# Two transposes of a round side by side, and weight sums in place, in a fused layer on one core

## The chip, the cores and the metric

The kernel runs on one core of a Trainium2 chip, in one launch. The metric is device time in microseconds (us), the median of three runs. TensorE multiplies matrices, ScalarE and VectorE work elementwise and read its results in PSUM, GpSimd works elementwise on SBUF alone, and SyncE issues most DMAs.

## The reference

The input x has 2048 tokens of 512 features. All matrices are float32.

```python
xn = _layernorm(x, axis=-1)
s = _A_ref(xn, A_wqkv, A_w_phi, A_wo)
g = _silu(_B_ref(xn, B_W_gate, B_W_up, B_W_down))
return x + s * g
...
# _A_ref: linear attention, 32 heads of 16; per head a 16x16 matrix w_phi
pq = jnp.einsum("bhsd,hdf->bhsf", q, w_phi)
pk = jnp.einsum("bhsd,hdf->bhsf", k, w_phi)
phi_q = jnp.concatenate([_softmax(pq, axis=-1), _softmax(-pq, axis=-1)], axis=-1)
phi_k = jnp.concatenate([_softmax(pk, axis=-1), _softmax(-pk, axis=-1)], axis=-1)
kv = jnp.einsum("bhsf,bhsd->bhfd", phi_k, v)
z  = jnp.einsum("bhsf->bhf", phi_k)
num = jnp.einsum("bhqf,bhfd->bhqd", phi_q, kv)
den = jnp.einsum("bhqf,bhf->bhq", phi_q, z)[..., None] + 1e-6
...
# _B_ref: (relu(xn @ W_gate) * (xn @ W_up)) @ W_down, 1376 hidden features
```

## The kernel before

**Numbers.** A float32 factor is split into a high part (fp32r, by a ScalarE copy) and a low part (the rest, by a subtraction on VectorE or GpSimd). `mm3` multiplies with three matmuls for each 128 rows: low by high, high by low, high by high. `fold` multiplies the key weights by the block-diagonal `w_phi`, so that one projection gives `pk`.

**Token tiles and rounds.** The 16 tiles of 128 tokens are taken in the order `order`; `pair(m)` is round m, m = 1 to 7, for the tiles n = 2m and n + 1. Around it stand a lead-in (weights, tiles 0 and 1) and the second part of the kernel (gate, up, down, queries, output), which begins at about 142 us and which the diff does not touch. In a round a later tile is normalized (`norm_stats`, `norm_scale`: VectorE and a power on GpSimd; `norm_apply`: a short VectorE operation and a ScalarE pass `xt`), transposed (`turn`: four TensorE transposes into `pxT`, a ScalarE copy of the high part and for an even tile one of the whole, `xf`) and completed (`turned`: VectorE subtracts the low part, and for an odd tile makes two sums `sb`). `sums_more`, `sums_hi` and `sums_lo` make from these the token sums S1 and S3 in `XT`.

**Seven products for eight.** From round 3 on (`FIRST`), the key and value projections of a pair of tiles are computed together as seven block products with sums of tokens and sums of weights (A11, S1, S2, A12, S3, A22, S4, in this order on TensorE). ScalarE copies `pk` to `px`, and TensorE goes on accumulating in `px`. The four weight sums T[0] to T[3] are made in `t_prep` in rounds 1 to 3: `PLAN` says at which place of which round each step runs. In "gc51" the letters are engine (g: GpSimd) and operation (c: combine, h: high part, l: low part), the digits which sum or combination and which half k. T[3] is the tile `th`.

**Order.** Every engine runs its instructions in the order of the program. Generators in `Clock` let out the other work (`q_sums` for the query weights `tq`, the preparations for the second part) when its own estimate of the engines' queues is short; `Q_AT` is the half round in which `q_sums` may begin. Buffers come from pools: `u8` has 2, `u4` 10, `u2` 40 (`t3`, `t4`, `vb`, `xt`, `xf`, `sb` and others), PSUM 8.

Of the kernel before, what the change touches and what calls it, by code (L numbers as in the profile page):

```python
# [19 lines left out]
KD = D // P  # L20
# [14 lines left out]
         *(((q, j), (q + 1, j)) for q in (6, 4) for j in range(2)), ((3, 0), (3, 1))]  # L35
LAST = [2 * q + j for q in QUERIES[1] for j in range(2)][-3:]
AHEAD, AT = (), ()
Q_TILES, Q_AT = ((), (1,)), 7
FIRST, SWAP = 3, 3
PLAN = {(0, "turned"): "gc51", (1, "split b"): "gc50", (1, "sums"): "gc01", (1, "scaled"): "gc11", (1, "mid"): "gc21", (1, "split a"): "gc00 sh01 gl01", (1, "turned"): "gc10", (2, "split b"): "sh20 sh11", (2, "sums"): "sh00 gc20", (2, "scaled"): "sh21 gl00", (2, "split a"): "gl20", (2, "turned"): "sh10 gc30 gl11", (2, "end"): "gl21 gl10", (3, "start"): "gc31 gc40 gc41", (3, "split b"): "sh30", (3, "sums"): "sh31 gl30 gl31"}  # L40

START = (14, 15)
TURN = 9
KV_AT = (2,4,6)
SUMS = 5
WO_WITH = (4, 5, 6, 7)
# [131 lines left out]
def layer_kernel(ctx: ExitStack, tc: tile.TileContext, x, wkT, wqT, wv, wo, wf, cst, out):  # L178
# [31 lines left out]
    def f32(t):  # L210
        return t.bitcast(F32)

    def add(engine, o, a, b, op=ALU.add):
        engine.tensor_tensor(o, a, b, op=op)
# [4 lines left out]
    def split(hi, lo, src, lo_engine=None):  # L219

        nc.scalar.activation(hi, src, AF.Copy)
        add(lo_engine or nc.vector, lo, src, f32(hi), ALU.subtract)
# [36 lines left out]
    def even_first(t):  # L259

        return t.rearrange("p (m a f) -> p a m f", a=2, f=DH)

    def by_parity(t):
        return t.rearrange("p (a m f) -> p a m f", a=2, f=DH)
# [19 lines left out]
    def fold(w, raw, k):  # L284

        p = ps(name="pfold")
        for j in range(KD):
            mm(p[:, j * P:(j + 1) * P], raw[:, j * P:(j + 1) * P], bd_sb[:, j, :], j == 0, True)
        return lambda: split(*map(by_parity, w[k]), even_first(p))


    mhalf = sb.tile([P, 96], F32, name="mhalf")[:, 0:2]
# [91 lines left out]
    def turned(n, p):  # L384
        lo_xt(n, p)
        if n % 2:
            sums_x(n, p)
# [1076 lines left out]
    def wv_lo(k):  # L1464
        add(nc.gpsimd, by_parity(WV[k][1]), even_first(wv_raw[:, k, :]), f32(by_parity(WV[k][0])), ALU.subtract)
# [22 lines left out]
    norm_vector_apply(1)  # L1488
    pk = project(0, WK, "pk")
    folds = fold_queries(0, 1)  # L1490
    for k in range(2):
        wv_hi(k)
        wv_lo(k)
    early = exponents(pk)
    folds[0]()
    folds[1]()
# [23 lines left out]
    def t_prep():  # L1520

        def four(name, whole, dt=F32R):
            if whole:
                t = u4((P, 2, D), name, dt)
                return [t[:, k] for k in range(2)]
            return [u2((P, D), name, dt) for k in range(2)]
        raw = [even_first(wv_raw[:, k, :]) for k in range(KD)]
        t3, t4, pairs = four("t3", False, F32), [], {}

        def source(i, k):  # L1530
            return raw[k + 2 * i] if i < 2 else by_parity((t3, t4)[i - 2][k])

        def combine(engine, k, i):
            if i == 5:
                add(engine, by_parity(t3[k]), raw[k + 2], raw[k], ALU.subtract)
            elif i < 2:
                add(engine, raw[k], raw[k], by_parity(f32(WK[k][i])), ALU.subtract)
            elif i == 2:
                add(engine, raw[k + 2], raw[k + 2], raw[k], ALU.subtract)
            else:  # L1540
                if not t4:
                    t4.extend(four("t4", False, F32))
                o, (wh, wl) = t4[k], WK[k + 2]
                if i == 3:
                    add(engine, by_parity(o), by_parity(f32(wh)), raw[k + 2], ALU.subtract)
                else:
                    add(engine, o, o, f32(wl))

        def hi(i, k):
            if i not in pairs:  # L1550
                if i < 3:
                    pairs[i] = list(zip(four(f"h{i}", not i), four(f"l{i}", not i)))
                else:
                    h = u8((P, 2, 2, D), "th", F32R)
                    pairs[i] = [(h[:, 0, j], h[:, 1, j]) for j in range(2)]
                T[i] = pairs[i]
            nc.scalar.activation(by_parity(T[i][k][0]), source(i, k), AF.Copy)

        def lo(engine, i, k):
            add(engine, by_parity(T[i][k][1]), source(i, k), by_parity(f32(T[i][k][0])), ALU.subtract)  # L1560
        def step(what):
            e, op, i, k = what
            engine, i, k = {"v": nc.vector, "g": nc.gpsimd, "s": None}[e], int(i), int(k)
            if op == "h":
                hi(i, k)
            elif op == "l":
                lo(engine, i, k)
            else:
                combine(engine, k, i)
        STEPS.append(step)  # L1570
# [74 lines left out]
    def pair(m):  # L1645

        n, c = 2 * m, cols(2 * m)
        at[0] = n

        def block(p, s, w, first):  # L1650
            mm3(p, lambda k: (XT[:, s, 0, k, c], XT[:, s, 1, k, c]), rows(w), range(2), first)
            pace.pump()
        if m <= NP // 2:
            pace.later(4, lambda: spill_x(n - 1))
        seven = m >= FIRST
        py = ps(name="pk")
        if seven:
            block(py, A11, WK[:2], True)
            px = ps(name="pk")
            nc.scalar.activation(px, py, AF.Copy)  # L1660
        else:
            mm3(py, xt_cols(n), rows(WK), range(KD))
        if m > 1:
            features_k(n - 1, *EB.pop(), engine=MULT[m > SWAP][1])
        t_steps(m, "start")
        pz = ps(name="pv")
        if seven:
            block(pz, S1, T[0], True)
            block(px, S2, T[1], False)
            va = u2((P, D), "va")  # L1670
            nc.scalar.activation(va, px, AF.Copy)
        else:
            mm3(pz, xt_cols(n + 1), rows(WV), range(KD))
        if m == 1:
            norm_apply(n + 4)
        else:
            features_split(n - 1)
        t_steps(m, "split b")
        news = [k for k in (n + 5, n + 6) if k < N]
        if news:  # L1680
            norm_stats(*news, bn=m > 2)
        if seven:
            block(py, A12, WK[2:], False)
        ea = exponents(py)
        if m > TURN and n + 3 < N:
            t = turn(n + 3)
        if seven:
            block(px, S3, T[2], False)
            vb = u2((P, D), "vb")
            nc.scalar.activation(vb, px, AF.Copy)  # L1690
            VH[n + 1] = u2((P, D), "v")
            add(nc.vector, by_head(VH[n + 1], True), by_head(pz), by_head(vb))
        else:
            vb = pz
        t_steps(m, "sums")
        if news:
            norm_scale(*news)
        t_steps(m, "scaled")
        pace.pump()
        at[0] = n + 1  # L1700
        if m <= TURN and n + 3 < N:
            t = turn(n + 3)
        exp_all(ea)
        if not seven:
            features_v(n + 1, vb)
        if n + 3 < N:
            turned(*t)
            sums_more(n + 3)
            sums_hi(n + 3, 0)
            if n + 7 < N:  # L1710
                load_x(n + 7)
        t_steps(m, "mid")
        query(n - 1)
        if m < SUMS:
            features_k(n, ea, py, engine=MULT[m > SWAP][0])
        if n + 3 < N:
            sums_hi(n + 3, 1)
            sums_lo(n + 3)
        if m >= SUMS:
            features_k(n, ea, py, engine=MULT[m > SWAP][0])  # L1720
        for k in news:
            norm_apply(k)
        pace.pump()
        features_split(n)
        t_steps(m, "split a")
        if m in KV_AT:
            kv_products(*range(KV_FROM.pop(), n))
            KV_FROM.append(n)
        pace.pump()
        if seven:  # L1730
            block(px, A22, T[3], False)
        else:
            px = project(n + 1, WK, "pk")
        eb = exponents(px)
        if seven:
            block(pz, S4, WV[2:], False)
            VH[n] = u2((P, D), "v")
            add(nc.vector, by_head(VH[n], True), by_head(pz), by_head(va))
        else:
            va = project(n, WV, "pv")  # L1740
        if n + 4 < N:
            t = turn(n + 4)
            if n + 8 < N:
                load_x(n + 8)
        exp_all(eb)
        t_steps(m, "turned")
        if n + 4 < N:
            turned(*t)
        if not seven:
            features_v(n, va)  # L1750
        EB.append((eb, px))
        query(n)
        t_steps(m, "end")
        pace.pump()
# [248 lines left out]
```

## Time and profile before

| | |
|---|---|
| three runs | 537.21, 538.18, 538.37 us (median 538.18) |
| profiled execution | 537.11 us, its span 535.3 us, granted clock 0.999 |
| TensorE (PE) | 530.0 us busy, 99% |
| weight loads (PEld) | 434.6 us, 81% |
| VectorE (DVE) | 388.0 us, 72% |
| ScalarE (ACT) | 261.2 us, 49% |
| GpSimd (POOL) | 415.6 us, 78% |
| chain that ended last | TensorE 84%, GpSimd 5%, ScalarE 4%, VectorE 3% |

A matmul's recorded length overlaps the next one's, so what TensorE achieves is read from the starts. All instructions stand under one source line, 77, a helper; they are told apart by tiles, "out<-in". "x4" at the end of a row of the order of time merges four like instructions; a bracket gives the engine's idle time ahead of it and what ended it.

### The profile page before, as it was taken

The numbers are of one execution on the slowest core, as the hardware profiler recorded it, in microseconds if no ns is written. First come the engines' busy times: TensorE is split into PE (matmuls) and PEld (weight loads), VectorE is DVE, ScalarE is ACT, GpSimd is POOL, SyncE is SP. The second block draws the span as 40 slices with busy tenths as digits, with TensorE's granted clock in tenths as the row PEclk, the third lists the DMA queues.
The fourth block names the chain that finished last, engine by engine and source line by source line (L and its number), as shares of the span: only waits on it lengthen the run. The fifth ranks groups of instructions, "written<-read, shape, count | busy, mean of one in ns | idle before, by whom it ended". The sixth has DMA issues, their size and how long they took to land.

```text
span 535.3 us, 9349 instructions
## 1 busy us (share of the span) xinstructions
PE 530.0 (99%) x3156; PEld 434.6 (81%) x3156; DVE 388.0 (72%) x624; ACT 261.2 (49%) x469; POOL 415.6 (78%) x366
## 2 busy tenths in 40 slices
PE   8999999999999999999999999999999999999997
PEld 8898887888887888788787887887887887878886
DVE  5987777688767328789898952898469468947565
ACT  3788767564524555535545142343635334345410
POOL 0669999867886999899899553595998997976760
PEclk9999999999999999999999999999999999999999
DMA  8439789557899758887679999998896788934774
GB/s 270 167 117 338 167 222 247 131 108 182 229 262 386 287 185 282 306 294 290 236 253 326 378 425 390 332 354 325 270 348 208 250 281 284 342 132 137 219 255 157
DMA packets 94991, 138.84 MB, mean 259 GB/s; under 512 B 8416, under 2 KB 46944, under 8 KB 94048
## 3 DMA queue, kind: packets, MB, share of 16 engines
q1 hardware_dynamic: 92784, 130.84, 71.6%
q0 software_dynamic: 2016, 7.34, 7.8%
q8 instruction: 25, 0.41, 0.3%
q14 instruction: 22, 0.18, 0.1%
q10 hardware_dynamic: 144, 0.07, 0.0%
HBM read 75.56 MB, written 58.46 MB: 250 GB/s over the span
## 4 chain that ended last, share of the span: by engine, by line
PE 84%; POOL 5%; ACT 4%; DVE 3%; issue 1%; DMA 1%; POOLq 0%; DVEq 0%; ACTq 0%
PE py L77 21%; PE pa L77 12%; PE pd L77 12%; PE pb L77 10%; PE pso L77 8%; PE pc L77 7%; PE pk L77 6%; PE pq L77 3%; PE pv L77 2%; PE pnum L77 2%; POOL XT L77 1%; PE pkv L77 1%; POOL t L77 1%; ACT junk L77 1%; POOL xf L77 1%
## 5 line engine op out<-in xcount | busy, mean ns | idle before, releaser
L77 PE MATMUL pa<-XT,wa 128*128 128x512 f32 x264 | 67.6, 391 | 0.0
L77 DVE TENSOR_TENSOR y<-py,y 128x512 f32<-128x512 f32 x68 | 46.1, 686 | 24.3 <-PE py L77 24.1
L77 PEld LDWEIGHTS pa<-XT,wa 128*128 128x128 f32 x264 | 49.3, 188 | 11.4 <-issue 1.2
L77 POOL TENSOR_TENSOR ez<-eq,zB 128x1024 f32<-128x1024 f32 x16 | 38.5, 2411 | 0.0
L77 PE MATMUL py<-fdh,hl 128*128 128x512 f32 x88 | 34.3, 390 | 0.0
L77 PE MATMUL py<-fdl,hh 128*128 128x512 f32 x88 | 34.2, 389 | 0.0
L77 PE MATMUL py<-fdh,hh 128*128 128x512 f32 x88 | 34.2, 389 | 0.0
L77 PE MATMUL pd<-XT,wc 128*128 128x512 f32 x132 | 33.8, 390 | 0.0
L77 PE MATMUL pd<-XT,wd 128*128 128x512 f32 x132 | 33.8, 390 | 0.0
L77 PE MATMUL pb<-XT,wb 128*128 128x512 f32 x132 | 33.6, 390 | 0.0
L77 PE MATMUL pc<-XT,wb 128*128 128x512 f32 x132 | 33.5, 389 | 0.0
L77 POOL TENSOR_TENSOR hl<-t,hh 128x512 fp32r<-128x512 f32 x20 | 25.7, 1294 | 9.5 <-ACT hh L77 9.3
L77 DVE TENSOR_TENSOR pb<-pb,t 128x512 f32<-128x512 f32 x17 | 11.9, 698 | 28.2 <-ACT pd L77 28.1
L77 PE MATMUL pq<-XT,wqh 128*128 128x512 f32 (+1 forms) x112 | 30.6, 360 | 0.0
L77 PE MATMUL pk<-wkh,XT 128*128 128x512 f32 x88 | 30.2, 394 | 0.0
L77 DVE TENSOR_REDUCE mx<-pk 128x32 f32<-128x512 f32 x32 | 20.5, 681 | 13.2 <-PE pk L77 13.2
L77 PEld LDWEIGHTS pb<-XT,wb 128*128 128x128 f32 x132 | 24.7, 188 | 5.5 <-ACT wc L77 0.4
L77 PEld LDWEIGHTS pd<-XT,wc 128*128 128x128 f32 x132 | 24.7, 188 | 5.5 <-issue 0.4
L77 PEld LDWEIGHTS pd<-XT,wd 128*128 128x128 f32 x132 | 24.7, 188 | 5.5 <-issue 0.4
L77 PEld LDWEIGHTS pc<-XT,wb 128*128 128x128 f32 x132 | 24.8, 188 | 5.2
L77 POOL TENSOR_TENSOR ol<-of,oh 128x512 fp32r<-128x512 f32 (+1 forms) x14 | 20.0, 1458 | 9.5 <-ACT oh L77 9.5
L77 ACT ACTIVATE pb<-pa 128x512 f32<-128x512 f32 x17 | 9.9, 585 | 33.8 <-PE pa L77 33.7
(249 smaller groups left out, 1612.8 us busy)
## 6 DMA issues: line engine op xcount, KB each, us to landing
xts<-XT SPq DMA_DIRECT2D x4, 1792.0 KB
zacc<-ek POOLq DMA_DIRECT2D x14, 512.0 KB, 5.6
XT<-xts SPq DMA_DIRECT2D x7, 1024.0 KB
rawg<-wf SPq DMA_DIRECT2D x22, 256.0 KB
ws<-wa SPq DMA_DIRECT2D x22, 256.0 KB
ws<-wb SPq DMA_DIRECT2D x22, 256.0 KB
ws<-wc SPq DMA_DIRECT2D x22, 256.0 KB
wa<-ws SPq DMA_DIRECT2D x22, 256.0 KB
```

Of the source, the lines that this page charges most:

```text
L77: return self.tc.keep_in_program_order(op(*a, **k))
```

## The change

Each round had one `turn` in its middle (tile n + 3) and one at its end (tile n + 4). Now, but for tile 5 in round 1, a round transposes n + 4 and n + 5 directly after each other at its end. `norm_apply` moves ahead of `features_k`. In the lead-in ScalarE copies each folded key weight whole into the buffer of its raw weights (`WHOLE`), and the four weight sums are made in place in the buffers `wv_raw` and `wk_raw` by eight additions; before there were twelve, with the high and low parts of the keys, and two pairs of tiles, `t3` and `t4`. `Q_AT` goes from 7 to 8.

```diff
-Q_TILES, Q_AT = ((), (1,)), 7
+Q_TILES, Q_AT = ((), (1,)), 8
-PLAN = {(0, "turned"): "gc51", (1, "split b"): "gc50", (1, "sums"): "gc01", (1, "scaled"): "gc11", (1, "mid"): "gc21", (1, "split a"): "gc00 sh01 gl01", (1, "turned"): "gc10", (2, "split b"): "sh20 sh11", (2, "sums"): "sh00 gc20", (2, "scaled"): "sh21 gl00", (2, "split a"): "gl20", (2, "turned"): "sh10 gc30 gl11", (2, "end"): "gl21 gl10", (3, "start"): "gc31 gc40 gc41", (3, "split b"): "sh30", (3, "sums"): "sh31 gl30 gl31"}
+PLAN = {(0, "turned"): "gc21", (1, "split b"): "gc20", (1, "sums"): "gc01", (1, "mid"): "gc11", (1, "split a"): "gc00 sh01 gl01", (2, "split b"): "sh20 sh21", (2, "sums"): "sh00 gc10", (2, "scaled"): "sh11 gl00", (2, "split a"): "gl20", (2, "turned"): "sh10 gc30 gl21", (2, "end"): "gl11 gl10", (3, "start"): "gc31  ", (3, "split b"): "sh30", (3, "sums"): "sh31 gl30 gl31"}
-TURN = 9
...
-        return lambda: split(*map(by_parity, w[k]), even_first(p))
+        def parts():
+            split(*map(by_parity, w[k]), even_first(p))
+            WHOLE[k] = lambda: nc.scalar.activation(by_parity(raw), even_first(p), AF.Copy)
+        return parts
...
     folds = fold_queries(0, 1)
+    for k in range(3):
+        WHOLE.pop(k)()
     for k in range(2):
         wv_hi(k)
         wv_lo(k)
+    WHOLE.pop(3)()
...
         raw = [even_first(wv_raw[:, k, :]) for k in range(KD)]
-        t3, t4, pairs = four("t3", False, F32), [], {}
+        whole = [by_parity(wk_raw[:, k, :]) for k in range(KD)]
+        pairs = {}
         def source(i, k):
-            return raw[k + 2 * i] if i < 2 else by_parity((t3, t4)[i - 2][k])
+            return (raw[k], whole[k], raw[k + 2], whole[k + 2])[i]
         def combine(engine, k, i):
-            if i == 5:
-                add(engine, by_parity(t3[k]), raw[k + 2], raw[k], ALU.subtract)
-            elif i < 2:
-                add(engine, raw[k], raw[k], by_parity(f32(WK[k][i])), ALU.subtract)
-            elif i == 2:
+            if i == 2:
                 add(engine, raw[k + 2], raw[k + 2], raw[k], ALU.subtract)
+            elif i == 0:
+                add(engine, raw[k], raw[k], whole[k], ALU.subtract)
+            elif i == 1:
+                add(engine, whole[k], whole[k], raw[k + 2])
             else:
-                if not t4:
-                    t4.extend(four("t4", False, F32))
-                o, (wh, wl) = t4[k], WK[k + 2]
-                if i == 3:
-                    add(engine, by_parity(o), by_parity(f32(wh)), raw[k + 2], ALU.subtract)
-                else:
-                    add(engine, o, o, f32(wl))
+                add(engine, whole[k + 2], whole[k + 2], whole[k], ALU.subtract)
...
-        if m > TURN and n + 3 < N:
-            t = turn(n + 3)
...
-        if m <= TURN and n + 3 < N:
+        if m == 1:
             t = turn(n + 3)
         exp_all(ea)
         if not seven:
             features_v(n + 1, vb)
+        if m == 1:
+            turned(*t)
         if n + 3 < N:
-            turned(*t)
             sums_more(n + 3)
             sums_hi(n + 3, 0)
...
         query(n - 1)
+        for k in news:
+            norm_apply(k)
         if m < SUMS:
             features_k(n, ea, py, engine=MULT[m > SWAP][0])
...
-        for k in news:
-            norm_apply(k)
...
         if n + 4 < N:
-            t = turn(n + 4)
+            t = turn(n + 4), turn(n + 5)
             if n + 8 < N:
                 load_x(n + 8)
         exp_all(eb)
         t_steps(m, "turned")
         if n + 4 < N:
-            turned(*t)
+            for x in t:
+                turned(*x)
```

## Rows read from the trace of the kernel before

**Rows 1.** The page's second part: granted clock in tenths, 40 equal slices.

```profile
PEclk9999999999999999999999999999999999999999
```

**Rows 2.** Waits of TensorE, whole span: us in total, times, longest.

```profile
PE pk L77 <- ACT pk L77: 0.2, 1, 0.2
```

**Rows 3.** The chain that ended last, round 5: start, us, what.

```profile
112.25 1.36 PE pk L77 x6
```

**Rows 4.** TensorE in order of time, rounds 3, 4 and 6: start, us, what.

```profile
77.39 1.70 PE L77 MATMUL pk<-th,XT 128*128 128x512 f32 x6
78.93 0.40 PE L77 MATMUL pv<-wvh,XT 128*128 128x512 f32 x1
...
86.01 0.39 PE L77 MATMUL pv<-h,XT 128*128 128x512 f32 x1
...
86.93 0.40 PE L77 MATMUL pk<-l,XT 128*128 128x512 f32 x1
...
117.80 0.39 PE L77 MATMUL pv<-h,XT 128*128 128x512 f32 x1
...
118.44 0.40 PE L77 MATMUL pk<-l,XT 128*128 128x512 f32 x1
```

**Rows 5.** TensorE in order of time, a lone run at round 3's end.

```profile
80.31 0.60 PE L77 MATMUL pxT<-ident,xt 128*128 128x128 f32 x4
80.67 0.48 PE L77 MATMUL pq<-XT,wql 128*128 128x512 f32 x1
80.98 0.40 PE L77 MATMUL pq<-XT,wqh 128*128 128x512 f32 x1
```

**Rows 6.** All engines in order of time, lead-in, a run of eight.

```profile
23.33 1.29 PE L77 MATMUL pxT<-ident,xt 128*128 128x128 f32 x8
...
23.96 0.42 PEld L77 LDWEIGHTS pxT<-ident,xt 128*128 128x128 f32 x4 [0.27 <-PE pxT L77]
...
24.38 0.48 PE L77 MATMUL pv<-wvh,XT 128*128 128x512 f32 x1
```

**Rows 7.** VectorE in order of time, round 3.

```profile
77.39 0.69 DVE L77 TENSOR_TENSOR XT<-pxT,XT 128x512 fp32r<-128x512 f32 x1 [0.19 <-ACT XT L77]
...
78.78 1.21 DVE L77 TENSOR_REDUCE sm<-ek 128x64 f32<-128x1024 f32 x1
...
82.00 1.28 DVE L77 TENSOR_REDUCE mx<-pk 128x32 f32<-128x512 f32 x2
```

**Rows 8.** ScalarE in order of time, rounds 3 and 4.

```profile
75.75 0.60 ACT L77 ACTIVATE vb<-pk 128x512 f32<-128x512 f32 x1 [1.32 <-POOL th L77]
...
84.50 1.06 ACT L77 ACTIVATE ek<-ek 128x1024 f32<-128x1024 f32 x1
...
85.94 0.59 ACT L77 ACTIVATE pk<-pk 128x512 f32<-128x512 f32 x1
```

**Rows 9.** GpSimd and TensorE in order of time, rounds 4 and 5.

```profile
92.23 2.84 POOL L77 TENSOR_TENSOR tq<-tab,tq 128x512 fp32r<-128x512 f32 x2
...
101.18 1.29 POOL L77 TENSOR_TENSOR XT<-xf,XT 128x512 fp32r<-128x512 f32 x1
...
103.46 0.39 PE L77 MATMUL pv<-h,XT 128*128 128x512 f32 x1
```

**Rows 10.** ScalarE in order of time, lead-in.

```profile
12.91 1.15 ACT L77 ACTIVATE wvh<-wvr 128x512 fp32r<-128x512 f32 x2 [1.97 <-DMA wvr<-wv]
15.12 0.66 ACT L77 ACTIVATE wqh<-pfold 128x256 fp32r<-128x256 f32 x2 [1.06 <-PE pfold L77]
```

**Rows 11.** All engines in order of time, round 1.

```profile
42.70 0.72 POOL L77 TENSOR_TENSOR lr<-lr,mhalf 128x2 f32<-128x2 f32 x1
...
45.10 0.48 PE L77 MATMUL pq<-XT,wql 128*128 128x512 f32 x1
...
46.11 0.63 ACT L77 ACTIVATE XT<-xf 128x512 fp32r<-128x512 f32 x1 [1.97 <-POOL xf L77]
...
46.65 0.80 ACT L77 ACTIVATE xt<-xt,lb,lr 128x512 f32<-128x512 f32 x1
```

More of the change, by code (lines that the diff above doesn't have):

```diff
@@ L288, in fold @@
             mm(p[:, j * P:(j + 1) * P], raw[:, j * P:(j + 1) * P], bd_sb[:, j, :], j == 0, True)
-        return lambda: split(*map(by_parity, w[k]), even_first(p))
+        def parts():
+            split(*map(by_parity, w[k]), even_first(p))
+            WHOLE[k] = lambda: nc.scalar.activation(by_parity(raw), even_first(p), AF.Copy)
+        return parts
+    WHOLE = {}
     mhalf = sb.tile([P, 96], F32, name="mhalf")[:, 0:2]
```

## The prediction

> **What bounds the kernel now.** I read the page's first two parts first: TensorE is busy for 99% of the span, at a granted clock of full speed (2.4 GHz) in every slice [rows 1], and the chain that ended last is TensorE for 84%. So time can come only from what TensorE is given to do, or from the moments in which it stands. The second view is the waits of TensorE: after the lead-in it names one alone, 0.2 us for ScalarE's copy `pk` [rows 2]. That view counts a wait only from the modelled end of a matmul, so the third reading is the starts of the matmuls in order of time. A 128x512 matmul starts every 0.227 us (six take 1.36 us) [rows 3]. Searched with that measure, the rounds hold three places where the step is longer for no change of shape [rows 4]: the block on `th` in round 3, whose six matmuls take 78.93 - 77.39 = 1.54 us, 0.18 too long; the block after the copy `px` in round 4, where two steps take 86.93 - 86.01 = 0.92 us instead of 0.454, 0.47 too long; and the same place in round 6, 118.44 - 117.80 = 0.64, 0.19 too long. Together 0.84 us. After the rounds I found none. That sum is the ceiling of what shorter queues elsewhere can bring in the rounds, and the reader is to see how small it is beside 535.3 us.
>
> **Two tiles in one run.** The work on TensorE stays: four transposes a tile, eight tiles in five runs now paired, (6,7) to (14,15). A lone run costs 80.98 - 80.31 = 0.67 us up to the second matmul behind it, of which 0.227 is a matmul's own: 0.44 us, with 0.36 in the run and 0.085 in the slow first step behind it [rows 5]. The lead-in already holds a run of eight [rows 6]: 24.38 - 23.33 = 1.05 us, less the 0.27 it waited for its data, is 0.78. So the second tile adds 0.42 and the pair saves 0.44 - 0.42 = 0.02 us. The bounds are 0 and, if each pair saved a whole slow step, 5 x 0.085 = 0.43 us. I take the run of eight, which is the same operation: 0.1 us.
>
> One rule of the Trainium skill speaks against longer runs. The trace first: the granted clock reads full speed in the lead-in's run of eight and in all lone runs [rows 1, 6]. The Trainium skill (TensorE: Matmul & The Clock Gate, Part 4: PE-mode transpose) says that transposes do not count as work for the clock gate; by it the clock might fall behind a doubled run, which would be a rival (below). By the trace the term is 0.
>
> **What moves with it.** ScalarE's copy and VectorE's subtraction and two sums for the odd tile leave the middle of a round and stand at its end. The middle gets 0.44 us shorter on TensorE, the end longer by the same. On VectorE the moved work in round 3 is 78.78 - 77.39 = 1.39 us [rows 7]. Behind it, without a gap, stand `features_k` and then the maxima of the second `px` at 82.00; `exp_all` starts on ScalarE at 84.50, and behind that the copy `px` which TensorE awaits, at 85.94 [rows 7, 8]. So the round 4 wait is VectorE's queue. Taking 1.39 us out of it lets this chain come up to 1.39 us earlier; against it stands the extra copy of the second tile on ScalarE ahead of `exp_all`, 0.59 us by the equal copy [rows 8]. Net 0.8 us earlier, where 0.47 is wanted: I take the whole 0.47. Bounds: nothing gained, if the earlier `norm_apply` (whose short VectorE operation now waits for GpSimd's power, ahead of `features_k`) eats the gain; 0.47 at most. In round 6 there is no query between the transposes and the first block, so the extra 0.59 us counts in full, and VectorE's gain only offsets it: I keep the wait of 0.19; bounds gone (0.19 gained) and 0.59 us worse.
>
> **Folded weights whole, sums in place.** Removed are four GpSimd additions of 128x512, about 1.29 us each by the row of that shape [rows 9], 5.2 us in rounds 1 to 3, and four buffers of the small pool (`t3`, `t4`). Added are four ScalarE copies of 0.59 us in the lead-in. Three stand ahead of the first `wvh`, where ScalarE idles 1.97 us for a DMA; the fourth stands behind the first two `wvh`, where it idles 1.06 us [rows 10]. 3 x 0.59 = 1.77 fits in 1.97, so they cost nothing; if the DMA came earlier, or they didn't fit, they would cost up to 4 x 0.59 = 2.4 us, since `wvh` feeds the first value projection. I take 0.
>
> In round 3 ScalarE's `vb` waited 1.32 us until GpSimd's `th` ended [rows 8]. `vb` does not read `th`; what it can want from it is the buffer of `t4` that `th` was the last to read. Behind `vb` stands the second `th` on ScalarE, behind that its low part on GpSimd, and for that the block in round 3 stood 0.18 us. With four buffers more, `vb` starts up to 1.32 us earlier, the block itself 0.44 earlier (no transposes ahead): 0.9 us to spare, so 0.18 is gained. If `vb` still waits, the block catches the same end 0.44 us sooner and loses 0.44 instead. I take the gain.
>
> The large pool has two buffers. `wk_raw` keeps one until round 3, so `th` takes that of `wv_raw` and `tq` waits for `wk_raw`. The last readers of both stand ahead on GpSimd's queue, which is 5.2 us lighter, so I take 0; a late reader would show as the 0.44 above. At a round's end two transposed tiles hold two of the eight PSUM buffers together; what else is held there then (`px`, `pz`, one query, the sums) makes five or six, so I take 0, and at most the second tile's slow step moves. None of the moved steps issues a DMA, and SyncE's queue keeps its order.
>
> **Query weight sums later, `norm_apply` earlier.** Both must not come late. The sums' GpSimd work, whose last pair of subtractions ran at 92.23 (2.84 us) [rows 9], goes on half a round longer. Nothing on TensorE reads `tq` until the second half, so their own lateness costs 0; what is queued behind them is a rival. In round 1 the second tile of the pair, 7, is now transposed at 45.10; before, its normalization ran at 46.65 [rows 11]. But GpSimd's power ended at 42.70 + 0.72 = 43.42, and ScalarE idled 1.97 us up to 46.11, that is from 44.14. With `norm_apply` ahead of `features_k` it can run from 44.14 to 44.94, 0.16 us ahead of need. I take 0; bound: if the order gains nothing, 46.65 + 0.80 - 45.10 = 2.35 us of wait.
>
> **The sum.** -0.10 (runs) - 0.47 (round 4) - 0.18 (round 3) + 0 + 0 = -0.75 us. The profiled execution took 537.11 us (span 535.3 and 1.8 around it), so 536.36; the median of the runs shown lies 1.07 above it, so the forecast is 538.18 - 0.75 = 537.4 us, 0.14% less. About 0.2%, 1.08 us, is what a measurement of this kernel can tell from no change (its three runs span 1.16 us).
>
> **Rivals.**
> A, nothing comes of it: the waits are renewed elsewhere. The queues are in order and short of slack, and the 0.44 us gained in the middle of each round brings every later need forward. For it: round 6 as above. Against it: 1.39 us leaves VectorE where its queue has no gap. Time 538.2, from 537.9 (the runs' 0.1 and the 0.18 gained) to 538.6 (the 0.44 of round 3 lost). Chance 0.17.
> B, slower: the sums moved on GpSimd. In round 5 the low part of the token sums ends at 101.18 + 1.29 = 102.47, and the first block that needs it starts at 103.46: about 1 us of slack [rows 9]. If the last pair of `tq` subtractions falls between, 2.84 us come in front: TensorE waits 2.84 - 0.99 = 1.85 us, for 538.18 - 0.75 + 1.85 = 539.3. It decides as soon as more than 1 us of the moved work stands there. Against it: GpSimd enters round 4 with 5.2 us less behind it, and the steps are let out only while its queue is short. Chance 0.09. The late normalization of tile 7, 2.35 us, would give 539.8; chance 0.04, since both its sources are done in time.
> C, faster than measurable: it takes all 0.84 us of waits, 0.43 from the runs, or something in the lead-in, whose own waits this reading doesn't price. -0.84 - 0.43 = -1.27 gives 536.9. Chance 0.16.
> D, the clock falls to its lower level, 1.2 GHz, in a longer run: each run of eight then takes 0.78 us more [rows 6], five of them 3.9, for 537.4 + 3.9 = 541.3. Every run of the kernel before, the one of eight too, ran at full speed [rows 1, 6], so 0.02. (It is the mechanism of the Trainium skill's page named above.)
>
> **How the numbers follow.** My own case has 0.52, of which I count 0.05 as measured over 0.2% faster, since 0.75 us is not far from 1.08. Faster: C and those 0.05, together 0.21. Within 0.2%: the other 0.47, A, and 0.03 for light forms of B, 0.67. Slower: what is left of B, 0.10, and D, 0.12. The range runs from C's 536.6 (its 536.9 less a third of a microsecond of spread) to 539.0, which takes in A and half of B. My case alone is 536.9 to 537.9.
>
> **What would show it.** Right: in `pxT` five runs of eight taking about 0.78 us; no step over 0.227 at the `th` block of round 3 and behind `px` in round 4; ScalarE's `vb` in round 3 directly behind its block; four copies from `pfold` in the lead-in with `wvh` still at 12.9; GpSimd 5 us less busy up to 80 us; TensorE's idle time after the rounds unchanged. Wrong: TensorE waiting in `pxT` for ScalarE's `xt` in round 1 or 4; a wait at the first S1 block of round 5 for GpSimd's `XT`; a longer step at `px` in round 6; a `wvh` that starts behind its DMA; a granted clock below full speed.

## The result, and the profile after

The changed kernel takes 538.62 us (median of 22 runs, 538.1 to 539.15) against 537.56 for the kernel before on the same chip: 1.0014 times, 95% interval 1.0009 to 1.0020. It is 1.06 us slower; 0.75 us faster was forecast, from a median of three runs (538.18) that lies 0.62 us above the median of 22. The profiled execution took 538.62 us too, with a span of 536.8.

Two views come first: the granted clock by slices, and the waits of TensorE. They answer to [rows 1] and [rows 2].

```profile
PEclk9999999999999999999999999999999999999999
```

```profile
PE pv L76 <- POOL XT L76: 1.5, 1, 1.5
...
PE pxT L76 <- ACT xt L76: 0.2, 1, 0.2
```

The granted clock never fell. Of the waits left out here both stand in the lead-in. New in the rounds are a wait of `pv` for GpSimd's token sums `XT`, and one of a transpose for ScalarE's normalized tile `xt`. The 0.2 us for `pk` is gone. TensorE in order of time shows the places of [rows 4] and [rows 5] and the two new ones (helper line 76 here, 77 before):

```profile
77.38 1.52 PE L76 MATMUL pk<-th,XT 128*128 128x512 f32 x6
78.74 0.39 PE L76 MATMUL pv<-wvh,XT 128*128 128x512 f32 x1
...
80.11 1.04 PE L76 MATMUL pxT<-ident,xt 128*128 128x128 f32 x8
80.90 0.47 PE L76 MATMUL pq<-XT,wql 128*128 128x512 f32 x1
...
86.24 0.39 PE L76 MATMUL pv<-h,XT 128*128 128x512 f32 x1
86.47 0.39 PE L76 MATMUL pk<-h,XT 128*128 128x512 f32 x1
...
98.21 0.60 PE L76 MATMUL pxT<-ident,xt 128*128 128x128 f32 x4
99.04 0.66 PE L76 MATMUL pxT<-ident,xt 128*128 128x128 f32 x4 [0.23 <-ACT xt L76]
...
103.41 0.39 PE L76 MATMUL pk<-wkh,XT 128*128 128x512 f32 x1
105.27 0.50 PE L76 MATMUL pv<-h,XT 128*128 128x512 f32 x1 [1.47 <-POOL XT L76]
105.61 0.40 PE L76 MATMUL pv<-l,XT 128*128 128x512 f32 x1
...
119.67 0.39 PE L76 MATMUL pv<-h,XT 128*128 128x512 f32 x1
...
120.32 0.40 PE L76 MATMUL pk<-l,XT 128*128 128x512 f32 x1
```

The `th` block of round 3 takes 1.36 us without a stall, and behind `px` in round 4 the step is 0.23: both gains came. The wait of round 6 stayed (120.32 - 119.67 = 0.65 for two steps). But in round 4 the second tile's transposes start 99.04 - 98.21 = 0.83 us behind the first's, which is 0.39 late, and the first block on S1 in round 5 starts 1.86 us behind its predecessor instead of 0.23, with a slow step of 0.34 behind it: 1.63 + 0.11 = 1.74 us.

Followed back from that block, the chain of the stretch from 76 to 108 us reads as follows (start, duration, what):

```profile
86.63 1.38 PE pk L76 x6
...
90.81 3.79 DMA pq<-pqs
...
94.70 0.61 ACT vb L76
...
95.33 0.69 DVE v L76
...
96.23 0.72 POOL lr L76
...
102.74 2.48 POOL XT L76 x2
...
105.27 1.65 PE pv L76 x6
```

TensorE leaves the chain at 86.63 + 1.38 = 88.01 us and comes back at 105.27. Between them stand a store of the queries to memory, ScalarE's `vb`, VectorE's `v`, GpSimd's power `lr`, more work on VectorE, and on GpSimd the feature product `ek` (100.81) with the low parts `XT` behind it. ScalarE and GpSimd in order of time show what that means (ScalarE answers to [rows 8], GpSimd to [rows 9]):

```profile
94.70 0.60 ACT L76 ACTIVATE vb<-pk 128x512 f32<-128x512 f32 x1 [4.62 <-DMA pq<-pqs]
...
96.66 1.14 ACT L76 ACTIVATE tq<-tab 128x512 fp32r<-128x512 f32 x2
...
98.18 1.51 ACT L76 ACTIVATE xt<-xt,lb,lr 128x512 f32<-128x512 f32 x2
```

```profile
96.23 0.71 POOL L76 TENSOR_TENSOR lr<-lr,mhalf 128x2 f32<-128x2 f32 x1 [3.73 <-DVE lr L76]
...
98.32 2.52 POOL L76 TENSOR_TENSOR tq<-tab,tq 128x512 fp32r<-128x512 f32 x2
100.81 1.94 POOL L76 TENSOR_TENSOR ek<-ek,rc 128x1024 f32<-128x1024 f32 x1
102.71 1.28 POOL L76 TENSOR_TENSOR XT<-sb,XT 128x512 fp32r<-128x512 f32 x1
103.95 1.26 POOL L76 TENSOR_TENSOR XT<-xf,XT 128x512 fp32r<-128x512 f32 x1
```

Two things have changed since [rows 9]. GpSimd now idles 3.73 us for `lr`, the time in which it made the `tq` subtractions before, and makes them (2.52 us) behind `lr`, in front of the feature product `ek` and the token sums' low parts. The chain leads to `ek` by way of VectorE, but `ek` starts at 100.81, as the second subtraction ends (98.32 + 2.52 = 100.84); in the first experiment below, with the subtractions out of the way, it starts at 99.18, before the VectorE work that the chain names (`ek` at 100.09 there). And `lr` itself is at 96.23 instead of 94.86, behind `vb`, which waited 4.62 us for a store whose data it neither reads nor writes: it wants the store's buffer, as the run with one buffer more shows below. SyncE's queue says why the store is late:

```profile
82.40 0.53 SPq L76 DMA_DIRECT2D xts<-XT  x1
85.38 5.85 SPq L76 DMA_DIRECT2D pq<-pqs  x2
```

The spill of the token sums `xts` (1.8 MB) is issued at 82.40, ahead of the two query stores (85.38 and 90.81); the instruction that issues the first of them is itself held for 5.37 us. By the trace's semaphore events the spill's last piece lands at 93.89, and the two stores right behind it, at 94.23 and 94.59, although 5.4 us lie between the starts of their issues. That agrees with the Trainium skill (DMA: Bandwidth & Descriptors, Queues, rings and completion order): on each DMA engine the descriptors of a queue are consumed in their order.

### The profile page after: what moved, and what is told of

The parts are those of the page before. It is cut to its first block, busy times and chain, and to the rows that moved or that the text cites. A ratio compares the mean times of both kernels' runs of the same rounds, so it can differ in the third digit from the quotient of the medians.

```text
span 536.8 us, 9342 instructions
## 1 busy us (share of the span) xinstructions
PE 529.5 (99%) x3156; PEld 434.4 (81%) x3156; DVE 387.9 (72%) x624; ACT 262.4 (49%) x473; POOL 410.6 (76%) x362
## 4 chain that ended last, share of the span: by engine, by line
PE 95%; DMA 1%; DVE 1%; POOL 1%; ACT 0%; issue 0%; SPq 0%; ACTq 0%
PE py L76 21%; PE pa L76 12%; PE pd L76 12%; PE pb L76 10%; PE pk L76 9%; PE pso L76 8%; PE pc L76 7%; PE pv L76 5%; PE pq L76 5%; PE pnum L76 2%; PE pfold L76 1%; PE pxT L76 1%; PE pkv L76 1%; DMA pq<-pqs 1%; DMA xt<-x 1%; POOL XT L76 0%
```

## The experiments

Theory Q: the query weight sums, moved behind `lr` on GpSimd, alone make the block late. Theory S: `vb`, whose buffer of the small pool is that of a late store, alone makes it late. Theory T: the paired turns cost it in another way. "Stretch" in the table is the time on TensorE from the first `pq` to the first `pa` of the profiled execution (142.58 - 27.19 before): all rounds, without the lead-in up to there, whose end varies between executions (27.2 to 28.3 us). Each ratio is to runs of the kernel before on the same chip (medians 537.34 to 537.56).

| kernel | median us | times before, 95% | stretch us | against before |
|---|---|---|---|---|
| before | 537.56 | 1 | 115.39 | 0 |
| changed | 538.62 | 1.0014 (1.0009 to 1.0020) | 116.74 | +1.35 |
| changed, sums let out as before | 537.11 | 0.9994 (0.9985 to 1.0002) | 115.17 | -0.22 |
| changed, spill later | 537.47 | 1.0001 (0.9992 to 1.0010) | 115.65 | +0.26 |
| paired turns alone | 538.18 | 1.0014 (1.0005 to 1.0023) | 116.15 | +0.76 |
| weights alone | 536.92 | 0.9991 (0.9982 to 1.0000) | 114.91 | -0.48 |
| changed, one buffer more | 537.49 | 1.0000 (0.9991 to 1.0009) | 115.46 | +0.07 |
| changed, low parts first | 536.64 | 0.9985 (0.9976 to 0.9994) | 114.65 | -0.74 |
| changed, spill later and low parts first | 536.49 | 0.9982 (0.9974 to 0.9991) | 114.43 | -0.96 |
| weights alone, spill later | 536.77 | 0.9983 (0.9974 to 0.9992) | 114.68 | -0.71 |
| before, spill later | 537.36 | 0.9999 (0.9990 to 1.0008) | 115.45 | +0.06 |
| weights alone, both edits | 536.57 | 0.9984 (0.9976 to 0.9993) | 114.69 | -0.70 |

**Sums let out as before.**

```diff
-Q_TILES, Q_AT = ((), (1,)), 8
+Q_TILES, Q_AT = ((), (1,)), 7
```

> The changed kernel with one number put back: the sums of the query weights are let out in the same place as before (Q_AT 7). Theory Q (the last sums of the query weights stand in GpSimd's queue ahead of the low parts of the token sums, and that alone makes the first block of round 5 late): the wait of 1.74 us there goes, so 1.5 to 1.8 us less than the changed kernel, about 536.9 (0.998 to 0.999 of the kernel before). Theory S (ScalarE's vb of round 4 waits 4.6 us for a query store that lands behind the spill of the token sums, and pushes everything behind it): vb still waits until about 94.7, and if that alone makes the block late, at least 1 us of its wait stays, and the time is within 0.7 us of the changed kernel, 537.9 to 538.6. Theory T (the paired turns themselves cost it): no difference, 538.6.

The wait at the S1 block went, as Q has it (one slow step of 0.34 us stayed), though `vb` still ran at 94.71. But not by S having no part: the last low part ended at 102.33 + 1.29 = 103.62 and the block started at 103.68, so the late `vb` had used the whole slack of 1 us of the kernel before. GpSimd in order of time:

```profile
92.12 1.59 POOL L76 TENSOR_TENSOR tq<-tab,tq 128x512 fp32r<-128x512 f32 x1
96.23 0.72 POOL L76 TENSOR_TENSOR lr<-lr,mhalf 128x2 f32<-128x2 f32 x1 [2.52 <-DVE lr L76]
...
99.18 1.94 POOL L76 TENSOR_TENSOR ek<-ek,rc 128x1024 f32<-128x1024 f32 x1 [0.83 <-DVE rc L76]
...
102.33 1.29 POOL L76 TENSOR_TENSOR XT<-xf,XT 128x512 fp32r<-128x512 f32 x1
```

And a new wait came. ScalarE in order of time:

```profile
87.62 0.63 ACT L76 ACTIVATE tq<-tab 128x512 fp32r<-128x512 f32 x1 [1.79 <-POOL tab L76]
88.45 0.63 ACT L76 ACTIVATE tq<-tab 128x512 fp32r<-128x512 f32 x1 [0.20 <-POOL tab L76]
88.99 0.58 ACT L76 ACTIVATE va<-pk 128x512 f32<-128x512 f32 x1
```

The copies for `tq` now stand ahead of `va` and wait for GpSimd's `tab`; `va` ends late, and TensorE, which goes on accumulating in `px`, starts its S3 block at 89.62 instead of 89.13: 0.49, with its slow step 0.60 us. So the half round later in the change is worth 0.60 and costs 1.74, and the 0.39 in the transposes, at other places.

**Spill later.** The spill is put off until the two query stores are issued.

```diff
-            pace.later(4, lambda: spill_x(n - 1))
+            pace.later(4 if m < 4 else 24, lambda: spill_x(n - 1))
```

> The changed kernel with one DMA moved: the spill of the token sums (1.8 MB) of rounds 4 on is issued behind the two query stores on SyncE's queue and not ahead of them. Theory S: the store lands some 8 us sooner, vb of round 4 starts right behind its block at about 91 instead of 94.7, and all that is queued behind it comes 3 to 3.5 us sooner; the 1.74 us at the first block of round 5 and the 0.39 us in the run of transposes at 98.2 both go: 536.4 to 536.8. Theory Q: the query sums still stand ahead of the low parts, so the block still waits 1.7 us: 538.6. Between them, if both must come together, it is also about 536.5, so this run alone does not tell S from both. Theory T: 538.6.

The stores, issued at 85.99 and 86.36, landed at 89.73 and 90.08 by the semaphore events, and `vb` ran at 91.35. The wait in the transposes went. Of the 1.74 us, 1.02 + 0.11 stayed, so neither theory is right as it stands: the moved sums alone make a wait, but not the whole of it, and the late `vb` alone makes none. The chain there (start, duration, what):

```profile
94.03 0.63 PE pkv L76 x32
...
94.75 0.69 DVE v L76
...
95.66 0.71 POOL lr L76
...
102.19 2.50 POOL XT L76 x2
...
104.74 1.65 PE pv L76 x6
```

With `vb` on time, VectorE's `v` is released only by the key-value products `pkv`, at 94.75. `lr` comes at 95.66 instead of 96.23; set against TensorE's own times, which are 0.59 us later here by the lead-in, that is 1.16 us earlier. The two sums still stand behind it.

**Each half of the change by itself.** The paired turns with the earlier `norm_apply`, without the rest; and the weights kept whole, the sums in place and the later query sums, without the paired turns.

```diff
 # paired turns alone: against the kernel before
-        if m <= TURN and n + 3 < N:
+        if m == 1:
             t = turn(n + 3)
...
-            t = turn(n + 4)
+            t = turn(n + 4), turn(n + 5)
...
 # weights alone: against the kernel before
-Q_TILES, Q_AT = ((), (1,)), 7
+Q_TILES, Q_AT = ((), (1,)), 8
...
+            WHOLE[k] = lambda: nc.scalar.activation(by_parity(raw), even_first(p), AF.Copy)
...
```

> The kernel before with only the paired turns and the earlier normalization; weight sums, folded weights and the place of the query sums as before. Theory Q: the query sums are where they were, so the first block of round 5 doesn't wait, and the time is that of the kernel before less what its round 4 wait (0.47) gives, plus up to 0.44 for the th block of round 3: 537.1 to 537.6. Theory S: the order of buffers is that of the changed kernel, vb of round 4 waits for the store, and the first block of round 5 waits 1 us or more: 538.2 to 539. Theory T: 538.4 or more with waits elsewhere, at the runs of transposes.

> The kernel before with only the folded weights kept whole, the sums in place and the query sums half a round later; the turns one tile at a time as before. Theory Q: the last query sums stand ahead of part of the low parts, and the first block of round 5 waits, 1 us or more: 538.2 to 538.8. Theory S: vb of round 4 doesn't wait for a store here, so the block waits little or nothing; the th block of round 3 gives 0.18, the px wait of round 4 (0.47) stays: 537.2 to 537.6. Theory T: no turns are paired, so nothing is lost: 537.4.

In the medians the turns alone lose about as much as the whole change (1.0014 each), in the stretch 0.76 of 1.35 us, but by neither theory's wait: the S1 block did not wait. The chain shows the same place as in the first experiment:

```profile
89.82 0.76 POOL tab L77
...
91.13 0.59 ACT va L77
...
91.76 1.66 PE pk L77 x6
```

The S3 block starts 1.12 us behind its predecessor instead of 0.23, about 1.0 us with its slow step. `vb` waited for the store here too (3.22 us, to 96.39), with the query sums in their old place and the old weight sums: it is the pairing that brings `vb` to that buffer. Two of the old stalls also stay without the new weight sums: the `th` block of round 3 takes 1.71 us, 0.35 too long, and the two steps behind `px` in round 4 take 0.72 us, 0.27 too long. (This profiled execution took 539.0 us, the longest of its runs, mostly by a later lead-in; the stretch leaves that out.)

The weights alone gained 0.48 us in the stretch, more than S expected, with almost no wait at the S1 block, though the query sums are let out half a round later here as well: letting them out later does not make the wait by itself, since here only one of the two falls in front of the low parts. The order of time of GpSimd:

```profile
94.44 0.71 POOL L76 TENSOR_TENSOR lr<-lr,mhalf 128x2 f32<-128x2 f32 x1 [3.37 <-DVE lr L76]
...
97.22 1.29 POOL L76 TENSOR_TENSOR tq<-tab,tq 128x512 fp32r<-128x512 f32 x1
98.48 1.94 POOL L76 TENSOR_TENSOR ek<-ek,rc 128x1024 f32<-128x1024 f32 x1
...
101.64 1.30 POOL L76 TENSOR_TENSOR XT<-xf,XT 128x512 fp32r<-128x512 f32 x1
```

`lr` is 1.79 us earlier than in the changed kernel, and one of the two `tq` subtractions stands in front instead of both. The low parts end at 102.94, and the block starts at 102.99, 0.08 late and with a slow step behind it. The wait at `px` in round 4 is gone here without any pairing.

**One buffer more** in the small pool.

```diff
-B8, B4, B2 = 2,10,40
+B8, B4, B2 = 2,10,41
...
```

> The changed kernel with 41 buffers in the small pool in place of 40 (room for it is made by a 96-column scratch tile cut to two columns and one reciprocal buffer of GpSimd's in place of two). All buffers behind the first turn of the pool shift by one, and vb of round 4 no longer takes the one that a query store reads. Theory S (vb held by the store is the cause): vb runs at about 91, and as far as the addition v behind it isn't held by another buffer, the power lr runs by 95.7 or sooner and the 1.74 us at the first block of round 5 falls to 1.0 or to nothing: 536.5 to 537.5. Theory Q (the last two query sums in GpSimd's queue are the cause by themselves): the wait stays at 1.7: 538.6. Rival (the single reciprocal buffer makes VectorE wait): a new wait, 538 or more.

`vb` ran at 90.97, without the store. That shows that its wait was for a buffer. But `v` behind it waited on VectorE:

```profile
94.26 0.69 DVE L76 TENSOR_TENSOR v<-pv,vb 128x512 f32<-128x512 f32 x1 [2.17 <-ACT tq L76]
```

The bracket names ScalarE, but by the semaphore events the second query store landed at 94.08, 0.18 us before `v` starts, the same distance as in the kernel before (93.79 and 93.97). So the store's buffer went from `vb` to `v`, and this run took only part of the lateness away. `lr` on GpSimd came at 95.17, and the block still waited 0.90 + 0.11 us. No wait of the single reciprocal buffer appeared on TensorE's path.

**Low parts first, alone and with the spill later.**

```diff
-SUMS = 5
+SUMS = 4
```

> The changed kernel with the two low parts of the token sums ahead of the 1.94 us feature product on GpSimd in round 4 (one constant, 5 to 4). vb is as late as before and the query sums stay in front. What is left is arithmetic on GpSimd's queue: the low parts end at 105.21 - 1.94 = 103.27, the first block of round 5 wants them at 103.64, so its wait of 1.74 us goes whole; the 0.39 in the run of transposes stays: 536.8 to 537.0. If the feature product, now 2.6 us later, is itself awaited, a new wait stands at the next products and the time is 537.5 or more. If the wait is not of GpSimd's queue at all, 538.6.

> The changed kernel with both the spill behind the two query stores and the low parts ahead of the feature product. Both waits should go, the 1.74 at the first block of round 5 and the 0.39 in the run of transposes, with round 6's 0.2 left: 538.6 - 2.1 = 536.5, 0.998 of the kernel before, and 0.4 less than with the low parts alone. If the spill moved later holds something else up (the loads of tokens behind it), 537 or more.

The whole wait went with this one constant. GpSimd, changed kernel with the low parts first:

```profile
98.22 2.52 POOL L76 TENSOR_TENSOR tq<-tab,tq 128x512 fp32r<-128x512 f32 x2
...
101.97 1.28 POOL L76 TENSOR_TENSOR XT<-xf,XT 128x512 fp32r<-128x512 f32 x1
103.22 1.93 POOL L76 TENSOR_TENSOR ek<-ek,rc 128x1024 f32<-128x1024 f32 x1
```

The low parts end at 103.25 and the block starts at 103.55, unwaited; nothing on TensorE waits for `ek`. The time, 536.64 us, lies below the 536.8 to 537.0 that were expected with the 0.39 us in the transposes kept: in this profiled execution the store landed earlier (`vb` waited 4.26 us instead of 4.62), and the run of eight at 98.39 took 0.96 us, 0.17 too long. With both edits the kernel takes 536.49 us, 1.0 us less than the one before, the fastest median here; it is not told apart from the low parts alone (536.64).

**Controls.** The spill later without the paired turns, in the weights alone and in the kernel before; and the weights alone with both edits.

> The kernel before with the folded weights kept whole, the sums in place, the query sums half a round later (no paired turns), and the spill behind the two query stores. The parts without the paired turns gave 0.9991; what the store still held there is 0.08 us at the first block of round 5 only, so: 536.7 to 537.0, no difference from the same without the spill moved. If it is below 536.6, the spill cost something that the steps of TensorE didn't show.

> The kernel before with the spill of rounds 4 on behind the two query stores, nothing else. In the kernel before the addition v of round 4 waited 1.82 us for the store, but no step of TensorE in round 5 was longer for it. If the store matters only through the paired turns (its lateness was within the slack of about 1 us), nothing changes: 537.3 to 537.7. If the spill costs something by itself, in the kernel before too, 536.9 or less.

> The weight part without the paired turns, the spill behind the two query stores, and the low parts of the token sums ahead of the feature product on GpSimd. Without the paired turns the low parts of round 4 were already in time, so the order on GpSimd should give nothing more: 536.7 to 536.9, as without it. It is run beside the same two edits on the paired turns (536.49, 0.9982), to see whether the paired turns are worth anything once their wait is gone: 0.05 us by the steps of the runs of eight, less than these runs can tell.

The first two came out as expected; the third, 536.57 us, lies 0.13 below its expected 536.7 to 536.9, less than these runs can tell. In the kernel before, the later spill frees `v` (92.85, without a wait, although this lead-in ended 0.72 us later; 93.97 before) and changes nothing in the time: there the store's lateness lay within the slack.

## Why the prediction was wrong

**The step that failed** is the end of "Query weight sums later", with its weight in rival B: "nothing on TensorE reads `tq` until the second half, so their own lateness costs 0", and against B "GpSimd enters round 4 with 5.2 us less behind it". GpSimd was lighter, by 4.0 us instead of 5.2 (43.67 us busy from 24 to 80 us, 47.66 before), but that was no help: it stood idle 3.73 us for `lr`, the last `tq` pair came after this gap and not in it, and 2.52 us stood in front of the low parts. That is rival B, at its place and nearly at its price (1.63 us and a slow step, forecast 1.85). The prediction had its threshold too, 1 us of moved work, and gave it 0.09. What it did not see is what eats the slack at the same time. It followed the buffer ring of the small pool for `vb` in round 3, where it gains, and not for round 4, where the pairing brings `vb` to the buffer of a query store behind a 1.8 MB spill. SyncE's queue kept its order, as forecast; what changed is who waits for the store: before it was `v` on VectorE, at 93.97, now it is `vb` on ScalarE, at 94.70, with `v` behind it at 95.33. The lateness of `lr` (1.37 us) and the sums in front together make the wait: without the moved sums it is 0, with `vb` on time and the moved sums it is 1.0, with the moved sums and no pairing 0.1, and with the low parts ahead 0. What the earlier `norm_apply` adds was not run by itself; it stands in every kernel with the paired turns.

The measured 538.62 us lies inside the stated 536.6 to 539.0, but by luck: the forecast's own case, 536.9 to 537.9, was a gain, and the range was counted from 538.18.

**Round 4, -0.47: right in size, wrong in its cause.** The wait went, but the weights alone remove it. In that kernel `vb` no longer waits for `th` in round 3, the work on VectorE moves up by 1.08 us (the maxima of `px` at 80.92 against 82.00 in [rows 7]), and ScalarE's copy runs at 85.04 instead of 85.94. With the turns alone 0.27 us of the wait stays. The 1.39 us that the pairing took off VectorE bought less than forecast: in the changed kernel VectorE then waited 1.37 us for GpSimd's `lr` ahead of `lb`, the bound named for the earlier `norm_apply`, and the copy ran at 85.31.

**Round 3, -0.18: right.** `vb` starts at 74.86 straight behind its predecessor, and the `th` block takes 1.36 us. **Round 6, 0.19 kept: right.**

**The runs, -0.10: too small.** A run of eight costs 80.90 - 80.11 = 0.79 us up to the next matmul, as forecast from [rows 6], and none waits in round 1 (tile 7 is in time). Two kernels that differ in the pairing and the place of `norm_apply` (both with the later spill and the low parts first) have stretches of 114.43 and 114.69: 0.26 us less with it, inside the bound of 0.43 (one profiled execution of each). The rows show where: the run of eight costs 0.08 us more than two lone runs (0.35 and 0.36), but the slowness behind a lone run is more than its first step, which is all that the forecast counted. The twelve query matmuls of round 3's first half take 77.39 - 74.55 = 2.84 us behind a lone run in the kernel before and 77.38 - 74.66 = 2.72 in the changed one, where none stands ahead of them (their first matmul, before and changed):

```profile
74.55 0.48 PE L77 MATMUL pq<-XT,wql 128*128 128x512 f32 x1
...
74.66 0.39 PE L76 MATMUL pq<-XT,wql 128*128 128x512 f32 x1
```

Together that saves 0.04 us a pair. In the times (536.49 and 536.57) it does not show.

**Not forecast:** the 0.39 us in the transposes at 98.21. The second tile's `xt` on ScalarE (98.18) stands behind `vb` and behind the two `tq` copies (1.14 us), and the paired run wants it straight behind the first tile. It went with the spill later, and with the sums let out as before.

**Lead-in, 0: right.** The first `pv` follows the first `pk` 7.47 us later, 7.48 before. **Clock:** full speed in every slice, runs of eight included, so the lower level of rival D did not come. No run here shows an effect of the Trainium skill's sentence on transposes (TensorE: Matmul & The Clock Gate, Part 4: PE-mode transpose).

The stretch grew by 1.35 us. The rows give 1.74 + 0.39 - 0.46 - 0.18 - 0.26 = +1.23; the remaining 0.12 stands in round 4: the four transposes behind the wait at 99.04 take 0.41 us instead of 0.36, and the key-value products ahead of 95.35 take 1.99 (from 93.36) instead of 1.92 before (94.11 to 96.03).

## What to carry to other kernels

Price a moved piece of work twice: in the queue it leaves, where it may have filled an idle gap for nothing, and in the queue it joins, where it stands in front of something. A ring of buffers has to be followed through every round when the order of allocations changes: here a buffer last read by a store made ScalarE stand 4.62 us until the store had landed behind the 1.8 MB ahead of it on its queue. A delay that fits into 1 us of slack by itself still uses it up: the late `vb` alone cost the S1 block nothing and the moved sums alone 1.0 us, both together 1.6. The cheapest repair was a third thing, the order of the work behind them.

## What the runs showed of the hardware

A 128 KB store issued at 90.81, 8.4 us behind a 1.8 MB spill on the same queue, landed at 94.59, 0.70 us behind the spill's last piece; SyncE's instruction for the store ahead of it took 5.37 us, from 85.38 to 90.75; with the spill behind them, two such stores landed 3.7 us after their issue. In the paired runs the eight transposes start 0.109 us apart across both tiles.
